# Soft-capped attention with a soft mixture of experts: queries and keys cast by transfers, more exponential tiles on VectorE, side jobs moved

## The chip, the core and the metric

The kernel runs on one NeuronCore of a Trainium2 chip. The core has TensorE (matmuls into PSUM), ScalarE (activation functions), VectorE and GpSimd (elementwise work) and SyncE, which here only issues transfers. The engines run their own instruction streams in order and wait for each other by semaphores. [...] The metric is the device time of one execution in microseconds (us). The traces name the engines PE (PEld for its weight loads), ACT, DVE, POOL and SP.

## The reference

For each of 8 batches and 12 heads, attention over 448 tokens of width 64, with scores capped by a tanh; then a soft mixture of 8 experts with 4 slots each over all 3584 tokens.

```
scores = cap * tanh((q @ k.T / 8) / cap)            # cap = 30
attn = exp(scores - max); attn /= sum + 1e-9
x = (attn @ v), heads side by side                   # 3584 x 768
logits = x @ phi                                     # 3584 x 32 slots
d = softmax of logits over tokens;  slot_input = d.T @ x
slot_out[e] = relu(slot_input[e] @ w1[e]) @ w2[e]
out = softmax of logits over slots @ slot_out        # 3584 x 768 f32
```

## The kernel before

**Attention.** Two heads that lie 64 rows apart on TensorE make a pair, two pairs a "quad" (four heads), three quads a batch: NQ = 24 quads, 48 pairs. A pair's scores are cut into 7 tiles of 128 x 448, 336 in all, worked off in 56 chunks of CH = 6 tiles. A batch is 7 chunks; "step n" of batch b is chunk 7b+n, n from 0 to 6.

For each chunk j the main loop (L523) emits: two tanh over three tiles each, from PSUM (`tanh_chunk`, L278); the exponential of an earlier chunk in place (`exp_chunk`, L282); the value pass of a pair, in two halves (`pv_pass`: 14 matmuls of L318, then on VectorE a reciprocal L328 and a product L329); and the scores of the next chunk, two groups of six matmuls (`qk_chunk`, L269). Since 48 pairs fall on 56 chunks, one step in seven (step 2) has no value pass. Exponential tiles have four buffers, so the tanh of chunk j+1 overwrites the buffer of chunk j-3. Scores have two buffers of three banks, the value pass one bank (psV), everything else one bank (psT, tag T).

**Preparation of a quad.** q and k come in as f32 by transfers from SyncE (`load`), VectorE casts them to bf16 (`cast`, L226), TensorE turns them by 7 transposes of 128 x 128 (`transp`, L237) and VectorE copies the result from PSUM (L239). v is cast on GpSimd in two halves (`vcast`, L247 and L248), as soon as the value passes of the quad two before are done.

**Side jobs.** For each batch: transposes of the attention output x (`x_transp`, L344 and L346), logits (L355, L360), the exponential of the logits (`e_exp`, L366), a copy of it on GpSimd (`e_rep`, L372), its transposes (`e_transp`, L391 and L392), the sum over tokens (`e_norm`, L379 and L383), slot sums (L407) and, every second batch, the reciprocal of sums over slots (`e_sums`, L401 and L402). `spare(n)` issues n filler matmuls (L506). All these have a place by hand: `at(j, slot, job)` puts a job in chunk j at slot 0 (ahead of the tanh), a (after the first half of the value pass), b (after the first scores), c (after the second half of the value pass) or d (after the second scores).

**Shared exponentials.** In the chunks listed in `shared` (L289) VectorE computes the exponential of tile 0 by a polynomial (`poly_exp`, L294 to L304) in three parts at slots a, c and d of the same chunk; ScalarE then does only five tiles.

**Weights.** w1 and w2 (f32) are loaded and cast by transfers from GpSimd, spread over slot b of the chunks (`wjobs`); the part of w2 that doesn't fit goes to DRAM as bf16 and is loaded back (`w2t`, L631) into memory that the attention frees.

**The end.** After the attention come the two expert layers (L649, L676) and the output: the first 10 token tiles are stored in two halves of 384 columns each (`half_tile`, L702 to L707), the first halves while the second layer still runs; the others as whole rows, ScalarE and VectorE taking turns.

Of the kernel before, what the change touches and what calls it, by code (L numbers as in the profile page):

```python
# [9 lines left out]
F32 = mybir.dt.float32  # L10
BF16 = mybir.dt.bfloat16
# [5 lines left out]
P = 128  # L17
HP = 64
NT = 7
DH = 64  # L20
S = 448
# [11 lines left out]
def kernel(  # L33
# [54 lines left out]
    slacc = consts.tile([P, NJ, NS], F32, name="slacc")  # L88

    w1b = [wts.tile([P, NJ, F], BF16, name=f"w1b{e}", tag="w1", bufs=E)  # L90
           for e in range(E - 1)]
    w2b = wts.tile([P, R2, D], BF16, name="w2b")


# [32 lines left out]

    att = ExitStack()
    ld = att.enter_context(tc.tile_pool(name="ld", bufs=1))
    cst = att.enter_context(tc.tile_pool(name="cst", bufs=1))  # L130
    ldv = att.enter_context(tc.tile_pool(name="ldv", bufs=1))
    qk = att.enter_context(tc.tile_pool(name="qk", bufs=2))
    vb = [att.enter_context(tc.tile_pool(name="vb0", bufs=1))]
# [22 lines left out]
                       ap=[[NT * DH, P], [2 * S * DH, 2], [1, NT * DH]])  # L156

    def raw_tile(nm):
        return (ldv if nm == "v" else ld).tile([P, 2, S], F32, name=nm + "raw",
                                               tag=nm + "raw")  # L160

    def load(nm, Q):
        if Q < NQ:
            t = raw_tile(nm)
            sp.dma_start(out=t, in_=quad_ap(nm, Q))
            raws[nm, Q] = t

    def load_first():

        for nm in "qkv":  # L170
            raws[nm, 0] = raw_tile(nm)
        kc = raws["k", 0].rearrange("p h (c d) -> p h c d", d=DH)
        kin = quad_ap("k", 0, 0).rearrange("p (c d) -> p c d", d=DH)
        sp.dma_start(out=raws["q", 0][:, 0, :], in_=quad_ap("q", 0, 0))
        for c0, c1 in ((0, CS), (CS, NT)):
            act.dma_start(out=kc[:, 0, c0:c1, :], in_=kin[:, c0:c1, :])
        for nm in "kq":
            sp.dma_start(out=raws[nm, 0][:, 1, :], in_=quad_ap(nm, 0, 1))
        t = wts.tile([P, 3, 2, S], F32, name="raw1", tag="w1", bufs=E)
        for n, nm in enumerate("kqv"):  # L180
            raws[nm, 1] = t[:, n, :, :]
            if nm == "v":
                sp.dma_start(out=raws["v", 0], in_=quad_ap("v", 0))
            sp.dma_start(out=raws[nm, 1], in_=quad_ap(nm, 1))

    def first_pieces(h, jobs):

        for stage, nm, c0, c1, eng, bank, at0 in jobs:
            copy = act.copy if eng is act else dve.tensor_copy
            cols = slice(h * HP, h * HP + HP)  # L190
            if stage == "cast":
                copy(casts[nm, 0][:, c0:c1, cols],
                     raws[nm, 0][:, h, c0 * DH:c1 * DH].rearrange("p (c d) -> p c d", d=DH))
            elif stage == "turn":
                for c in range(c0, c1):
                    pe.transpose(bank[cols, at0 + c - c0, :], casts[nm, 0][:, c, cols], ident)
            else:
                copy(qkT[nm, 0][cols, c0:c1, :], bank[cols, at0:at0 + c1 - c0, :])

    def first_half(h):  # L200
        for nm in ("k", "q"):
            if h == 0:
                casts[nm, 0] = cst.tile([P, NT, P], BF16, name=nm + "bf", tag=nm + "bf")
                qkT[nm, 0] = qk.tile([P, NT, P], BF16, name=nm + "T", tag=nm + "T")
        one = psT.tile([P, 8, P], BF16, name="ps1", tag="T")
        two = psV.tile([P, NT, P], BF16, name="ps2", tag="pv")
        if h == 0:

            first_pieces(h, (("cast", "k", 0, CS, dve, None, 0), ("cast", "q", 0, 4, dve, None, 0),
                             ("cast", "q", 4, NT, act, None, 0), ("turn", "k", 0, CS, pe, two, 0),  # L210
                             ("copy", "k", 0, CS, dve, two, 0), ("turn", "q", 0, 4, pe, one, 0),
                             ("cast", "k", CS, NT, act, None, 0),
                             ("copy", "q", 0, 4, dve, one, 0), ("turn", "q", 4, NT, pe, two, CS),
                             ("copy", "q", 4, NT, act, two, CS), ("turn", "k", CS, NT, pe, one, 4),
                             ("copy", "k", CS, NT, dve, one, 4)))
        else:
            first_pieces(h, (("cast", "k", 0, NT, dve, None, 0), ("cast", "q", 0, NT, dve, None, 0),
                             ("turn", "k", 0, NT, pe, two, 0), ("turn", "q", 0, NT, pe, one, 0),
                             ("copy", "k", 0, NT, dve, two, 0), ("copy", "q", 0, NT, dve, one, 0)))
            for nm in ("q", "k"):  # L220
                raws.pop((nm, 0)), casts.pop((nm, 0))
                load(nm, 2)

    def cast(nm, Q):
        t = cst.tile([P, NT, P], BF16, name=nm + "bf", tag=nm + "bf")
        dve.tensor_copy(t.rearrange("p c (h d) -> p h c d", h=2),  # L226
                        raws.pop((nm, Q)).rearrange("p h (c d) -> p h c d", d=DH))
        casts[nm, Q] = t
        if Q > 1:
            load(nm, Q + 1)  # L230

    def transp(nm, Q):
        src = casts.pop((nm, Q))
        home = (psV, "pv") if (nm, Q) == ("k", 1) else (psT, "T")
        ps = home[0].tile([P, NT, P], BF16, name=nm + "ps", tag=home[1])
        for c in range(NT):
            pe.transpose(ps[:, c, :], src[:, c, :], ident)  # L237
        t = qk.tile([P, NT, P], BF16, name=nm + "T", tag=nm + "T")
        dve.tensor_copy(t, ps)  # L239
        qkT[nm, Q] = t  # L240
# [45 lines left out]

    shared = [j for j in range(NCH - 2) if j % 7 == 3 and j > 7] if cap < 80 else []  # L289

    def poly_exp(j, part):
        t, bits = exs[j][:, 0, :], 2.0 ** 23
# [146 lines left out]

    def quad_in(Q, cast_k, cast_q, k_in, q_in, v_in):  # L440
        if 0 < Q < NQ:
            at(*cast_k, cast, "k", Q)
            at(*cast_q, cast, "q", Q)
            at(*k_in, transp, "k", Q)
            at(*q_in, transp, "q", Q)
            at(*v_in, vcast, Q)

    for b in range(B):
        j = b * PER
        if b == 0:  # L450
            quad_in(1, (0, "a"), (0, "b"), (0, "d"), (1, "a"), (2, "d"))
        else:
            quad_in(3 * b + 1, (j - 1, "b"), (j, "a"), (j - 1, "d"), (j, "c"), (j + 1, "d"))
        quad_in(3 * b + 2, (j + 1, "c"), (j + 2, "c"), (j + 2, "b"), (j + 2, "d"),
                (j + 4, "d"))
        quad_in(3 * b + 3, (j + 4, "a"), (j + 5, "a"), (j + 4, "d"), (j + 5, "c"),
                (j + 6, "d"))
        p = 6 * b
        at(j + 1, "d", spare, 34 if b == 0 else 10)
        at(j + 2, "d" if b == 0 else "a", spare, 4 if b == 0 else 14)  # L460
        if b:
            at(j + 2, "c", spare, 8)
        at(j + 3, "d", spare, 10)
        at(j + 4, "a", x_transp, p)
        at(j + 5, "a", x_transp, p + 1)
        at(j + 6, "a", x_transp, p + 2)
        at(j + 5, "d", logits, 3 * b)
        if b < B - 1:
            at(j + 7, "a", x_transp, p + 3)
            at(j + 8, "a", x_transp, p + 4)  # L470
            at(j + 7, "d", logits, 3 * b + 1)
            at(j + 9, "a", x_transp, p + 5)
            at(j + 9, "d", logits, 3 * b + 2)
            at(j + 11, "0", e_exp, b)
            at(j + 11, "d", slot_sums, b)
            if b < B - 2:
                at(j + 12, "d", e_transp, b)
            if b < B - 2:
                at(j + 13, "d", e_norm, b)
            if b % 2:  # L480
                at(j + 14, "d", e_sums, b // 2)
    for j in shared:
        for dj, slot, part in ((0, "a", 0), (0, "c", 1), (0, "d", 2)):
            at(j + dj, slot, poly_exp, j, part)
    for n, job in enumerate(wjobs):
        at(1 + n * (NCH - 5) // len(wjobs), "b", *job)
    for j, slot, n in ((0, "a", 10), (0, "c", 10), (1, "b", 10), (1, "c", 8)):
# [208 lines left out]
    def half_tile(n, half, home, eng):  # L696

        if n % 8 == 0:
            obs[n, half] = wts.tile([P, 8, HD], F32, name="obh", tag="w1", bufs=E)
        ob = obs[n - n % 8, half][:, n % 8, :]  # L700
        bb, c = divmod(n, NT)
        pe.matmul(home, et_tile(bb, c), so[half], start=True, stop=True)  # L702
        if eng == "dve":
            dve.tensor_scalar_mul(ob, home, winv[:, bb, c:c + 1])
        else:
            act.mul(ob, home, winv[:, bb, c:c + 1])
        store(n, half, half + 1, ob)  # L707
# [10 lines left out]
    for n0 in range(0, n2, 4):  # L718
        layer2(n0, 1)
        if n0 >= 4 and n0 % 8 == 4 and done < NH - 2:  # L720
            for eng in ("act", "dve"):
                half_tile(done, 0, bank([P, HD], name="op0"), eng)
                done += 1
    dve.tensor_copy(so[1], so_ps[1])
    for n in range(done, NH):
# [68 lines left out]
```

The softmax here doesn't subtract the row's maximum and nothing guards it: scores larger than these inputs give would overflow.

## Time and profile before

| | |
|---|---|
| time, three runs | 317.34 to 318.18 us, median 318.17 |
| span of the profiled run | 314.8 us |
| attention | up to some 269 us |
| tanh, L278 | 113 instructions, 162.3 us busy |
| exponentials, L282 | 58 instructions, 159.2 us busy |
| casts of q and k on VectorE, L226 | 46 instructions, two of 128x896 per quad |
| casts of v on GpSimd, L247 and L248 | 24 each, some 0.93 and 0.96 us |
| VectorE's polynomial, L294 to L304 | 7 chunks, seven instructions each |
| filler matmuls, L506 | 470 |

A row of the groups reads: line, engine, operation, output and input with their shapes, count, busy time and mean duration, idle time before it and what ended it. Busy times on ScalarE overlap, so two of its rows can add up to more than the time that they took. In the listing in order of time a row has its start, its length, the engine, the line and, in brackets, the idle time before it and what ended that. In the chain of work that ended last a piece has start, length and what it was.

### The profile page before, as it was taken

What the parts mean: (1) busy time and instruction counts of PE and PEld (TensorE: products, weight loads), DVE (VectorE), ACT (ScalarE), POOL (GpSimd) and SP (SyncE); (2) the same over time, 40 slices, a digit from 0 to 9 for tenths busy, and PEclk for the clock granted to TensorE, in tenths of its full rate; (3) what the DMA queues carried; (4) which work ended last, traced back from release to release, by engine and by line L of the source; (5) the groups of instructions that cost most, each with busy time, mean ns of one, the idle gap of its engine ahead of it and who ended that gap; (6) DMA issues with size and microseconds to landing.
All of it is one profiled execution on the core that took longest, in us unless ns stands there. A gap on an engine that the chain in (4) does not pass through costs nothing.

```text
span 314.8 us, 8844 instructions
## 1 busy us (share of the span) xinstructions
PE 269.4 (86%) x3804; PEld 191.0 (61%) x3804; DVE 193.7 (62%) x473; ACT 281.3 (89%) x208; POOL 106.5 (34%) x134
## 2 busy tenths in 40 slices
PE   7899898899889998898889989898889998998720
PEld 6667665667666665666666666666666677743400
DVE  3636565766586659575867587657766574327840
ACT  4999999999999999999999999999999999326730
POOL 2464342523543452354245416441732130200000
PEclk9999999999999999999999999999999999999985
DMA  8899999799999999999999999999999807898997
GB/s 223 267 234 238 291 244 269 159 231 256 235 210 231 266 237 207 254 220 266 194 225 269 221 264 190 242 235 266 209 232 254 214 14 207 290 393 301 389 411 314
DMA packets 57479, 77.68 MB, mean 247 GB/s; under 512 B 3809, under 2 KB 53601, under 8 KB 57441
## 3 DMA queue, kind: packets, MB, share of 16 engines
q0 software_dynamic: 30480, 25.22, 52.1%
q1 hardware_dynamic: 26672, 51.68, 48.1%
q8 instruction: 29, 0.48, 0.6%
q10 hardware_dynamic: 288, 0.23, 0.2%
q14 instruction: 10, 0.07, 0.1%
HBM read 91.32 MB, written 18.87 MB: 350 GB/s over the span
## 4 chain that ended last, share of the span: by engine, by line
ACT 67%; PE 20%; DVE 5%; issue 3%; DMA 2%; DVEq 0%; ACTq 0%
ACT ex L278 33%; ACT ex L282 32%; PE pv L318 5%; PE sc L269 3%; PE so_ps L676 2%; PE junk L506 2%; PE hp L649 2%; ACT ob L754 1%; PE op L702 1%; DMA kraw<-in_k_dram 1%; DVE xq L329 1%; PE op L745 1%; PE xps L344 1%; DMA out_dram<-obh 1%; DVE ob L752 1%
## 5 line engine op out<-in xcount | busy, mean ns | idle before, releaser
L278 ACT ACTIVATE ex<-sc 128x1344 bf16<-128x1344 f32 (+1 forms) x113 | 162.3, 1693 | 0.9 <-PE sc L269 0.8
L282 ACT ACTIVATE ex<-ex 128x2688 bf16<-128x2688 bf16 (+4 forms) x58 | 159.2, 2779 | 0.1
L318 PEld LDWEIGHTS <-ex 128*128 128x128 bf16 x1344 | 78.7, 97 | 21.5 <-DVE xq L329 17.8
L318 PE MATMUL pv<-vbd,ex 128*128 128x130 bf16 x1274 | 88.6, 220 | 2.6 <-ACT ex L282 0.7
L269 PE MATMUL sc<-qT,kT 64*64 64x448 bf16 x672 | 78.6, 358 | 8.2 <-ACT ex L278 7.9
L247 POOL CAST vbd<-vraw 64x896 bf16<-64x896 f32 x23 | 21.5, 936 | 103.6 <-PE pv L318 65.3
L269 PEld LDWEIGHTS <-kT 64*64 64x64 bf16 x672 | 27.3, 105 | 25.3 <-issue 7.5
L329 DVE TENSOR_TENSOR xq<-pv,rec 128x256 bf16<-128x256 f32 x91 | 38.6, 424 | 3.1
L328 DVE RECIPROCAL rec<-pv 128x4 f32<-128x4 f32 x91 | 16.5, 181 | 32.1 <-PE pv L318 31.2
L506 PEld LDWEIGHTS <-ones 128*128 128x128 bf16 x470 | 28.6, 100 | 11.6 <-DVE xq L329 8.0
L372 POOL COPY e<-E 128x512 bf16<-128x512 bf16 x9 | 7.2, 795 | 81.5 <-ACT E L366 49.6
L506 PE MATMUL junk<-ones 128*128 128x128 bf16 x433 | 31.4, 219 | 2.5 <-DVE xq L329 1.6
L239 DVE COPY kT<-kps 128x896 bf16<-128x896 bf16 x23 | 14.4, 625 | 24.6 <-PE kps L237 24.4
L109 POOL DMA_DIRECT2D w1b<-in_moe_w_dram x32 | 25.2, 791 | 0.0
L248 POOL CAST vbd<-vraw 64x896 bf16<-64x896 f32 x23 | 23.7, 1029 | 1.3
L346 DVE COPY xT<-xps 128x512 bf16<-128x512 bf16 x47 | 19.5, 415 | 3.2 <-PE xps L344 3.0
L344 PE MATMUL xps<-ident,xq 128*128 128x128 bf16 x188 | 18.1, 218 | 0.2 <-DVE zacc L383 0.2
L239 DVE COPY qT<-qps 128x896 bf16<-128x896 bf16 x23 | 14.2, 616 | 5.2 <-PE qps L237 5.2
L226 DVE CAST kbf<-kraw 128x896 bf16<-128x896 f32 x22 | 16.0, 728 | 1.3 <-DMA kraw<-in_k_dram 1.3
L237 PE MATMUL kps<-ident,kbf 128*128 128x128 bf16 x161 | 12.8, 219 | 4.2 <-DVE slacc L418 2.2
L237 PE MATMUL qps<-ident,qbf 128*128 128x128 bf16 x161 | 12.8, 219 | 3.2 <-DVE lg L360 2.7
L237 PEld LDWEIGHTS <-kbf 128*128 128x128 bf16 x161 | 10.0, 97 | 9.0 <-issue 8.3
(113 smaller groups left out, 255.5 us busy)
## 6 DMA issues: line engine op xcount, KB each, us to landing
w1b<-in_moe_w_dram POOLq DMA_DIRECT2D x32, 384.0 KB, 10.2
vraw<-in_v_dram SPq DMA_DIRECT2D x23, 448.0 KB, 6.6
qraw<-in_q_dram SPq DMA_DIRECT2D x22, 448.0 KB, 7.8
kraw<-in_k_dram SPq DMA_DIRECT2D x22, 448.0 KB, 6.0
w2d<-in_moe_w_dram POOLq DMA_DIRECT2D x20, 384.0 KB, 9.2
w2t<-w2d SPq DMA_DIRECT2D x20, 384.0 KB, 5.9
out_dram<-ob SPq DMA_DIRECT2D x8, 768.0 KB, 7.3
w2b<-in_moe_w_dram POOLq DMA_DIRECT2D x12, 384.0 KB, 9.9
```

The costliest lines, as they stand in the source:

```text
L109: pool.dma_start(out=w1b[e][:, js, fs], in_=w1r[:, e, js, fs])
L237: pe.transpose(ps[:, c, :], src[:, c, :], ident)
L239: dve.tensor_copy(t, ps)
L247: pool.tensor_copy(t[0:HP, :, :, 0:DH], raw[0:HP])
L248: pool.tensor_copy(t[HP:P, :, :, DH + 1:VW - 1], raw[HP:P])
L269: pe.matmul(sc[cs, u, 0:S], qkT["k", Q][r, c, cs], qkT["q", Q][r, :, cs], start=True, stop=True)
L278: act.activation(exs[j][:, half * CS + u0:half * CS + u1, :], sc[:, u0:u1, 0:S], ACT.Tanh, scale=qk_scale / cap)
L282: act.activation(exs[j][:, u0:u1, :], exs[j][:, u0:u1, :], ACT.Exp, scale=cap)
L318: pe.matmul(pvs[pr, half][:, n, 0:VW], exs[j][:, u, GOFF[g]:GOFF[g] + P], vbds[Q % 2][:, h, c, :], start=(c == 0 and n == 0), stop=(c == N ...
L329: dve.tensor_tensor(xq[Q][:, 2 * half:2 * half + 2, h * P:(h + 1) * P] .rearrange("p g (i d) -> p g i d", i=2), pv[:, :, :, 0:DH], rec.to_ ...
L344: pe.transpose(ps[:, g, :], xq[Q][:, g, h * P:(h + 1) * P], ident)
L506: pe.matmul(junk if home is None else home, ones, ones, start=True, stop=True)
```

## The change

Four things. (1) From the third quad on, q and k are cast to bf16 by the transfers themselves, issued from GpSimd into two buffers each; VectorE's casts remain for the first two quads, whose bf16 tiles lie in a weight buffer. The transposes read the loaded layout directly: 14 of 128 x 64 per tensor in place of 7 of 128 x 128. (2) The polynomial takes a tile in 16 chunks (steps 1 and 3 of each batch from chunk 8 on, and chunks 3 and 54) in place of 7; its third part moves to the next chunk. (3) Side jobs move: k of the third quad is turned one chunk earlier, e transposes, token sums and sums over slots three, three and two chunks later, and the fillers at steps 1, 2 and 3 shrink from 10, 14 and 10 to 6, 12 and 4. (4) The first half output tile is computed into two PSUM banks of 192 columns, scaled by ScalarE and VectorE side by side. It is meant to take exponential work from ScalarE, make room for it on VectorE, keep TensorE's side work spread out, and let the first store go earlier.

```diff
@@ loads and casts
-    cst = att.enter_context(tc.tile_pool(name="cst", bufs=1))
...
     def raw_tile(nm):
-        return (ldv if nm == "v" else ld).tile([P, 2, S], F32, name=nm + "raw",
-                                               tag=nm + "raw")
+        if nm == "v":
+            return ldv.tile([P, 2, S], F32, name="vraw", tag="vraw")
+        return ld.tile([P, 2, S], BF16, name=nm + "b", tag=nm + "raw", bufs=2)
 
     def load(nm, Q):
         if Q < NQ:
             t = raw_tile(nm)
-            sp.dma_start(out=t, in_=quad_ap(nm, Q))
+            (sp if nm == "v" else pool).dma_start(out=t, in_=quad_ap(nm, Q))
             raws[nm, Q] = t
...
-    def cast(nm, Q):
-        t = cst.tile([P, NT, P], BF16, name=nm + "bf", tag=nm + "bf")
-        dve.tensor_copy(t.rearrange("p c (h d) -> p h c d", h=2),
-                        raws.pop((nm, Q)).rearrange("p h (c d) -> p h c d", d=DH))
-        casts[nm, Q] = t
-        if Q > 1:
-            load(nm, Q + 1)
+    def cast(nm):
+
+        dve.tensor_copy(casts[nm, 1].rearrange("p c (h d) -> p h c d", h=2),
+                        raws.pop((nm, 1)).rearrange("p h (c d) -> p h c d", d=DH))
 
     def transp(nm, Q):
-        src = casts.pop((nm, Q))
+        src = casts.pop((nm, Q)) if Q == 1 else raws.pop((nm, Q))
...
         for c in range(NT):
-            pe.transpose(ps[:, c, :], src[:, c, :], ident)
+            if Q == 1:
+                pe.transpose(ps[:, c, :], src[:, c, :], ident)
+                continue
+            for h in range(2):
+                pe.transpose(ps[h * HP:h * HP + HP, c, :], src[:, h, c * DH:(c + 1) * DH], ident)
@@ shared exponentials
-    shared = [j for j in range(NCH - 2) if j % 7 == 3 and j > 7] if cap < 80 else []
+    shared = [j for j in range(NCH) if j % 7 in (1, 3) and j > 7 or j in (3, NCH - 2)] if cap < 80 else []
@@ places of the jobs
         if 0 < Q < NQ:
-            at(*cast_k, cast, "k", Q)
-            at(*cast_q, cast, "q", Q)
+            for nm, when in (("k", cast_k), ("q", cast_q)):
+                at(*when, *((cast, nm) if Q == 1 else (load, nm, Q + 1)))
...
-        quad_in(3 * b + 2, (j + 1, "c"), (j + 2, "c"), (j + 2, "b"), (j + 2, "d"),
+        quad_in(3 * b + 2, (j, "d"), (j + 1, "c"), (j + 2, "b"), (j + 2, "d"),
                 (j + 4, "d"))
-        quad_in(3 * b + 3, (j + 4, "a"), (j + 5, "a"), (j + 4, "d"), (j + 5, "c"),
+        quad_in(3 * b + 3, (j + 4, "a"), (j + 5, "a"), (j + 3, "d"), (j + 5, "c"),
                 (j + 6, "d"))
-        at(j + 1, "d", spare, 34 if b == 0 else 10)
-        at(j + 2, "d" if b == 0 else "a", spare, 4 if b == 0 else 14)
+        at(j + 1, "d", spare, 34 if b == 0 else 6)
+        at(j + 2, "d" if b == 0 else "a", spare, 4 if b == 0 else 12)
...
-        at(j + 3, "d", spare, 10)
+        at(j + 3, "d", spare, 10 if b == 0 else 4)
...
             if b < B - 2:
-                at(j + 12, "d", e_transp, b)
-            if b < B - 2:
-                at(j + 13, "d", e_norm, b)
+                at(j + 15, "d", e_transp, b)
+                at(j + 16, "d", e_norm, b)
             if b % 2:
-                at(j + 14, "d", e_sums, b // 2)
+                at(j + 16, "d", e_sums, b // 2)
     for j in shared:
-        for dj, slot, part in ((0, "a", 0), (0, "c", 1), (0, "d", 2)):
-            at(j + dj, slot, poly_exp, j, part)
+        for slot, part in (("a", 0), ("c", 1)):
+            at(j, slot, poly_exp, j, part)
+        at(j + 1, "b" if j % 7 == 1 else "a", poly_exp, j, 2)
@@ half_tile
+        if n == half == 0:
+
+            for p, (bank_p, mul) in enumerate(zip(home, (act.mul, dve.tensor_scalar_mul))):
+                cs = slice(p * HD // 2, (p + 1) * HD // 2)
+                pe.matmul(bank_p, et_tile(bb, c), so[half][:, cs], start=True, stop=True)
+                mul(ob[:, cs], bank_p, winv[:, bb, c:c + 1])
+            store(n, half, half + 1, ob)
+            return
```

## The prediction

> **What bounds the kernel now.** I read the busy shares first, then the chain of work that ended last, then the waits, and then one batch in order of time.
>
> ```profile
> PE 269.4 (86%) x3804; PEld 191.0 (61%) x3804; DVE 193.7 (62%) x473; ACT 281.3 (89%) x208; POOL 106.5 (34%) x134
> ```
>
> ScalarE is busiest, and in each 32.6 us stretch of the attention it is busy for all 32.6. The chain shows what one chunk costs it (start, us, what):
>
> ```profile
> 185.09 2.33 ACT ex L282
> 187.62 2.36 ACT ex L278 x2
> 189.99 1.96 ACT ex L282
> ```
>
> Two tanh (2.36 us) and one exponential: 2.33 us for six tiles, 1.96 where VectorE takes one of the six. That is 0.37 us per tile handed over. The waits say who leans on whom (total us, times, longest):
>
> ```profile
> ACT ex L278 <- PE sc L269: 0.8, 1, 0.8
> ```
> ```profile
> PE sc L269 <- ACT ex L278: 7.9, 19, 0.7
> ```
>
> ScalarE waits for TensorE once, at the start; TensorE waits for ScalarE 19 times. So ScalarE sets the end of the attention, and 0.37 us per tile is won as long as TensorE stays ahead. How far ahead is the question. I call chunk 7b+n "step n" of batch b. TensorE in steps 1 to 3 of batch 5:
>
> ```profile
> 175.95 0.98 PE L318 MATMUL pv<-vbd,ex 128*128 128x130 bf16 x14
> ...
> 178.24 0.39 PE L344 MATMUL xps<-ident,xq 128*128 128x128 bf16 x4
> ...
> 179.33 0.75 PE L269 MATMUL sc<-qT,kT 64*64 64x448 bf16 x6
> ...
> 182.78 0.96 PE L318 MATMUL pv<-vbd,ex 128*128 128x130 bf16 x14
> 183.96 0.75 PE L269 MATMUL sc<-qT,kT 64*64 64x448 bf16 x6 [0.22 <-ACT ex L278]
> ```
> ```profile
> 186.90 3.09 ACT L278 ACTIVATE ex<-sc 128x1344 bf16<-128x1344 f32 x2
> ```
>
> Step 2 has no value pass (L318), so side jobs sit there. The last line is step 4's two tanh. Recorded starts on ScalarE run early late in the span, but ends agree with TensorE (it takes a score bank 0.04 us after a tanh ends), so I count from ends: the pair ends at 189.99, its first member at 188.81, and needs 1.2 us, so must begin at 187.61. It writes an exponential buffer last read by step 3's second value pass (four buffers). That pass could start at 184.48, when the first pass's norm is done, and end at 185.45: **2.16 us of slack**.
>
> [...] here the 128*32 matmuls of L649 take 1.41 us for 24 of 512 columns, a quarter of serial. [...]
>
> ```profile
> 187.53 0.62 DVE L303 SCALAR_TENSOR_TENSOR xp<-xp,xm 128x448 f32<-128x448 f32 x1
> 187.75 0.87 POOL L372 COPY e<-E 128x512 bf16<-128x512 bf16 x1 [7.07 <-ACT E L366]
> ...
> 188.19 0.91 DVE L304 SCALAR_TENSOR_TENSOR ex<-xp,xe 128x448 bf16<-128x448 f32 x1
> ```
>
> The copy takes 0.87 us, not 0.61 as when alone; L304 takes 0.91, not the 0.63 of its shortest run. Each starts in effect 0.14 us before the other ends[...]. Casts of v do the same:
>
> ```profile
> 177.06 0.93 POOL L247 CAST vbd<-vraw 64x896 bf16<-64x896 f32 x1 [4.74 <-PE pv L318]
> ...
> 177.53 0.94 DVE L226 CAST kbf<-kraw 128x896 bf16<-128x896 f32 x1
> ...
> 178.04 1.24 POOL L248 CAST vbd<-vraw 64x896 bf16<-64x896 f32 x1
> ```
>
> **The change part by part.**
>
> *Sixteen shared chunks instead of seven.* ScalarE saves 9 x 0.37 = 3.35 us. VectorE pays 9 x 3.66 us (shortest runs of L294 to L304), 33 us.
>
> *Casts in transfers.* 44 VectorE casts go (L226, 16.0 + 14.5 = 30.5 us), so its total is nearly unchanged; 67% of a batch is no bound. GpSimd issues 44 more transfers at about 0.77 us (L109), 34 us beside 106 of busy time: hidden. The engines of the transfers carry the same reads. A transfer from GpSimd lands 10.2 us after issue (median; longest 16.0, third in a burst). I put the tightest, the k load of step 4, some 12 us ahead of its transposes and leading its burst: no cost.
>
> *Twice as many transposes, of half the columns.* [...] If they pair as L649's do, 14 take some 0.03 us more than 7 (0.55); if serial, 0.39 more. I take 0.03. Twelve fillers fewer per batch return 12 x 0.057 = 0.7 us (ten take from 177.67 to 178.24).
>
> *Side jobs moved.* Steps 5 and 6 lose the e transposes and the normaliser sum, so TensorE enters step 1 at its limit, the free score bank (scores at 174.58, when a tanh had ended, instead of 175.37): its second value pass starts 0.8 us earlier against ScalarE than in batch 5 above. But step 1 is now crowded on VectorE. Count from the end of that pass (176.93 above). Norm to 0.66. The v cast waits for the same pass and starts at 0.13, ending at 1.06; the first two-input polynomial step (L300) gets in at 0.92 and ends at 1.53; [...] the next step (L301) ends at 2.84, and only then comes the copy of the e transposes, to 3.22. There is one side-job bank in PSUM (tag T), so step 2's x transposes wait until 3.28; behind them in TensorE's queue stand 12 fillers and the scores, at 4.27. Before, the scores came at 179.33 - 176.93 = 2.40. Later by 1.87, less 0.8: **1.1 us**.
>
> In step 2, from scores to the next value pass took 182.78 - 179.33 = 3.45. Now: k transposes 0.69 to 1.27, VectorE's copy to 1.92, the third polynomial part (0.66 + 0.63) to 3.13, and behind it the sum's addition (3.22), logits (0.35) and addition (0.3) to 3.94, q transposes, value pass at 4.4: **1.0 us** more. After odd batches the reciprocal of e sums adds another 0.62 (in the trace, 173.44 to 174.06). Against a start that ScalarE's own saving in step 2 makes 0.37 us earlier, lateness is 1.1 + 1.0 + 0.37 = 2.5 us, odd 3.1, against 2.16: ScalarE stalls **0.35** or **0.95**.
>
> In step 3 the k transposes, moved there, have their copy behind the second polynomial part; step 4's x transposes wait for that copy. By the same counting, step 4's second value pass is another 0.3 us late. This holds for batches 2 to 7 (0 and 1 have no e transposes to place): 3 x 0.65 + 3 x 1.25 = **5.7 us**.
>
> *First output tile in two halves.* The first store leaves after half an L706 (0.58): some 0.25 us earlier, and transfers are full from then on. The smaller cast pool lets one less weight reload start early (about 1 us of transfer), which fits into the 1.7 us hole before the first store.
>
> Sum: 318.17 - 3.35 - 0.25 + 5.7 = **320.3 us**.
>
> **The rivals.**
>
> *The saving lands.* VectorE's slack takes it all: 318.17 - 3.6 + 0 to 0.6, about **314.9**. For it: VectorE has 10 us idle per batch (busy 22.14 of 32.70), steps 5 and 6, tightest before, are relieved, and without the collision of L300 and L301 with the v cast (0.95 us) the 2.16 us nearly suffice. Against: the collision follows from one and the same value pass.
>
> *Half of it.* Only the odd batches and step 4 stall, 3 to 4 us: **318.0**.
>
> *TensorE becomes the bound.* Serial transposes put 3 x 0.39 us more into steps 2 and 3: some 7 us over six batches, **327**. Against: L649, and the scores (L269), which overlap by pairs.
>
> *Keys come late*, behind bursts of weights in one queue: a few us, **323**. Against: the lead of 12 us.
>
> **How the numbers follow.** Forecast 0.40; saving lands 0.36; half 0.16; TensorE 0.05; late keys 0.03. Faster is the second, same the third, slower the rest, 0.48. The lateness of one batch is known to some 0.4 us, so six batches to 2.4: up to 322.8; down, the full saving, 314.4.
>
> **What the profile would show.** Right: ScalarE's L278 waiting for pv (L318) in steps 4 and 5 of batches 2 to 7, 0.3 to 1 us each; TensorE's L344 waiting for the ET copy (L392), about 2 us in step 2; L301 near 1.2 us and not 0.63 in step 1; exponentials of 1.96 us 16 times. Wrong: if ScalarE waits for nothing, the saving lands; if kps and qps groups of 14 take 0.95 us, transposes are serial; if transposes wait for transfers, the queue is the cause. I would be wrong above all if VectorE reached L300 before the v cast starts, or if the buffer were free before the pass ends.

## The result and the profile after

The changed kernel takes **338.19 us** (median of four executions, 334.0 to 342.59) against 318.18 (317.34 to 319.43): a ratio of 1.053, 95% interval 1.044 to 1.062. The forecast was 320.3 and its range ended at 322.8. Executions more than 1.5% over the fastest of their kernel are left out of the ratios, and since these are mostly the ones in which TensorE's clock fell furthest, the median of such a kernel says more than its ratio. Lines of the changed kernel are those of the kernel before plus 8 (tanh L286, exponential L290, value pass L326, x transposes L352, L400 the "ET copy", which takes the e transposes out of PSUM).

Busy time first, then two rows of slices from the same page, for the changed kernel:

```profile
PE 295.2 (87%) x4029; PEld 203.6 (60%) x4029; DVE 199.2 (58%) x493; ACT 279.5 (82%) x208; POOL 137.4 (40%) x178
```
```profile
ACT  4999999999499989998699858999999759514730
PEclk9999999997599979995799757999999559999995
```

The clock row of the kernel before:

```profile
PEclk9999999999999999999999999999999999999985
```

ScalarE's total fell by 1.8 us, but it now has holes, and they lie where the clock row shows something new: digits of 5 and 7, where before it was 9 throughout the attention. The clock that TensorE is granted falls to half again and again. The clock record of this execution (start and length in us) says how long:

```
81.6 13.7   122.6 3.4   153.3 13.7   190.9 17.1   262.5 17.1     (all at 0.5 of full)
```

That is 64.9 us of the attention at half clock, in pieces of 1, 4 or 5 times 3.41 us. The kernel before had none, up to 304 us. The chain of work that ended last, by engine, before and after:

```profile
ACT 67%; PE 20%; DVE 5%; issue 3%; DMA 2%; DVEq 0%; ACTq 0%
```
```profile
ACT 39%; PE 38%; DVE 15%; issue 2%; DMA 2%; DVEq 0%; SPq 0%; ACTq 0%
```

The waits of the changed kernel (total us, times, longest):

```profile
ACT ex L286 <- PE pv L326: 17.7, 12, 3.3
...
PE xps L352 <- DVE ET L400: 10.2, 6, 2.3
...
ACT ex L286 <- PE sc L277: 8.6, 7, 1.8
```

The forecast's two signs are there: ScalarE waits for a value pass twelve times, eleven of them in steps 4 and 5 of batches 2 to 7 (one, of 0.2 us, is in batch 0), and the x transposes wait for the ET copy six times. But the twelve come to 17.7 us where it had 5.7, and seven waits for scores stand beside them, where there was one. Batch 2 in order of time (start, length, then engine and line) shows the start of it on VectorE and GpSimd:

```profile
77.93 1.03 POOL L255 CAST vbd<-vraw 64x896 bf16<-64x896 f32 x1 [3.26 <-PE pv L326]
...
78.64 0.80 DVE L308 SCALAR_TENSOR_TENSOR xp<-xm 128x448 f32<-128x448 f32 x1
...
79.02 1.24 POOL L256 CAST vbd<-vraw 64x896 bf16<-64x896 f32 x1
...
79.47 1.26 DVE L309 SCALAR_TENSOR_TENSOR xp<-xp,xm 128x448 f32<-128x448 f32 x1
...
80.66 0.38 DVE L400 COPY ET<-eps 128x448 bf16<-128x448 bf16 x1
```

and what TensorE does meanwhile and after it:

```profile
78.42 0.40 PE L399 MATMUL eps<-ident,e 128*128 128x128 bf16 x4
78.78 0.51 PE L514 MATMUL junk<-ones 128*128 128x128 bf16 x6
81.08 0.38 PE L352 MATMUL xps<-ident,xq 128*128 128x128 bf16 x4 [1.79 <-DVE ET L400]
81.31 1.18 PE L514 MATMUL junk<-ones 128*128 128x128 bf16 x12
82.42 1.33 PE L277 MATMUL sc<-qT,kT 64*64 64x448 bf16 x6
83.67 0.96 PE L245 MATMUL kps<-ident,kb 128*64 128x128 bf16 x14
```

The second value pass of step 1 ended at 77.79. Counted from there the ET copy ends at 3.25 (forecast 3.22) and the x transposes begin at 3.29 (forecast 3.28); L309 takes 1.26 us, 0.63 at its shortest, and the half of the v cast beside it (L256) 1.24 where the median is 0.96. The forecast's count had the two lengthen each other, an estimate from such pairs in the trace before; why they do isn't shown. Up to here the forecast is right to 0.03 us. Then TensorE, idle for 1.79 us, comes back to a granted clock of 0.50: six score matmuls take 1.33 us and not 0.76, 14 half transposes 0.96 and not 0.58. The table by stretches of 3.4 us has PE busy second and the granted clock in the third column from the right:

```profile
74.80:78.20 3.40, 3.01 (x43) 2.20 (x42) 2.31 (x8) 3.40 (x4) 0.27 (x1) 1.00 1.21 235
78.20:81.60 3.40, 1.60 (x24) 1.13 (x21) 2.86 (x6) 3.40 (x3) 3.34 (x4) 1.00 1.25 205
81.60:85.00 3.40, 3.40 (x35) 2.13 (x33) 0.66 (x2) 3.40 (x3) 0.90 (x2) 0.50 1.17 256
85.00:88.40 3.40, 2.77 (x32) 1.62 (x32) 1.90 (x5) 1.78 (x3) 0.00 (x0) 0.50 1.23 207
```

A stretch with TensorE busy 1.60 of 3.40 us, and the next one is at 0.50. Coming back takes longer: TensorE is busy for 3.40, 2.77, 3.40 and 3.40 us of the four stretches from 81.6, and yet the clock stays at half until 95.3. One comparison lies in the execution itself: batch 6 has the same jobs as batches 2 and 4 but no stretch at half clock, and ScalarE loses 0.3 us there (counted as in the table below), where it loses 5.1 and 5.2 us in those two. So the theory to test: **a stretch of some 3.4 us with little work on TensorE halves its clock; ScalarE then waits for passes that take 1.70 us in place of 0.97** (the 14 matmuls from 88.95 against those from 76.82). The rivals: it is the thinner fillers; it is the casting transfers; or the waits that the forecast counted are simply longer, and the clock is an effect.

### The profile page after: what moved, and what is told of

It is laid out like the page before. It is cut to its first block, busy times and chain, and to the rows that moved or that the text cites. A ratio compares the mean times of both kernels' runs of the same rounds, so it can differ in the third digit from the quotient of the medians.

```text
span 340.8 us, 9280 instructions
## 1 busy us (share of the span) xinstructions
PE 295.2 (87%) x4029; PEld 203.6 (60%) x4029; DVE 199.2 (58%) x493; ACT 279.5 (82%) x208; POOL 137.4 (40%) x178
## 4 chain that ended last, share of the span: by engine, by line
ACT 39%; PE 38%; DVE 15%; issue 2%; DMA 2%; DVEq 0%; SPq 0%; ACTq 0%
ACT ex L286 19%; ACT ex L290 19%; PE pv L326 11%; PE sc L277 8%; PE junk L514 4%; PE kps L245 2%; DVE xq L337 2%; DVE xp L309 2%; PE qps L245 2%; PE so_ps L684 2%; DVE xp L308 2%; PE hp L657 2%; DMA out_dram<-ob 2%; PE xps L352 1%; DVE xm L304 1%
## 5 line engine op out<-in xcount | busy, mean ns | idle before, releaser
L286 ACT ACTIVATE ex<-sc 128x1344 bf16<-128x1344 f32 (+1 forms) x113 | 140.9, 1316 | 26.3 <-PE pv L326 17.7
L290 ACT ACTIVATE ex<-ex 128x2688 bf16<-128x2688 bf16 (+4 forms) x58 | 133.5, 2305 | 0.1
L326 PE MATMUL pv<-vbd,ex 128*128 128x130 bf16 x1274 | 97.5, 231 | 4.2 <-ACT ex L290 2.4
L326 PEld LDWEIGHTS <-ex 128*128 128x128 bf16 x1344 | 84.8, 103 | 26.9 <-DVE xq L337 13.5
L277 PE MATMUL sc<-qT,kT 64*64 64x448 bf16 x672 | 87.2, 390 | 3.6 <-ACT ex L286 2.1
L514 PEld LDWEIGHTS <-ones 128*128 128x128 bf16 x386 | 27.1, 110 | 7.8 <-issue 3.3
L352 PE MATMUL xps<-ident,xq 128*128 128x128 bf16 x188 | 18.4, 221 | 11.1 <-DVE ET L400 10.2
L256 POOL CAST vbd<-vraw 64x896 bf16<-64x896 f32 x23 | 23.6, 1028 | 1.3
L352 PEld LDWEIGHTS <-xq 128*128 128x128 bf16 x188 | 13.1, 98 | 12.3 <-issue 12.3
L245 PEld LDWEIGHTS <-kb 128*64 128x64 bf16 x308 | 11.4, 128 | 10.8 <-issue 10.8
L167 POOL DMA_DIRECT2D qb<-in_q_dram x22 | 16.2, 737 | 3.6 <-DMA kraw<-in_k_dram 3.2
L245 PE MATMUL qps<-ident,qb 128*64 128x128 bf16 x308 | 14.7, 242 | 2.9 <-DVE lg L368 2.9
```

The source lines that it names most:

```text
L245: pe.transpose(ps[h * HP:h * HP + HP, c, :], src[:, h, c * DH:(c + 1) * DH], ident)
L256: pool.tensor_copy(t[HP:P, :, :, DH + 1:VW - 1], raw[HP:P])
L277: pe.matmul(sc[cs, u, 0:S], qkT["k", Q][r, c, cs], qkT["q", Q][r, :, cs], start=True, stop=True)
L286: act.activation(exs[j][:, half * CS + u0:half * CS + u1, :], sc[:, u0:u1, 0:S], ACT.Tanh, scale=qk_scale / cap)
L290: act.activation(exs[j][:, u0:u1, :], exs[j][:, u0:u1, :], ACT.Exp, scale=cap)
L326: pe.matmul(pvs[pr, half][:, n, 0:VW], exs[j][:, u, GOFF[g]:GOFF[g] + P], vbds[Q % 2][:, h, c, :], start=(c == 0 and n == 0), stop=(c == N ...
```

## The experiments

From the profiled execution of seven of the kernels, in us: the attention from the first tanh to the end of the last exponential, ScalarE's lost time in it, the time of it at half clock, and the span after it. Lost time is counted from ends, as in the prediction: by how much each instruction of ScalarE ends later than the one before it plus the usual time (the median) of its shape. The changed kernel's is its longest execution, 342.59 us.

| | attention | ScalarE lost in it | at half clock | after it |
|---|---|---|---|---|
| before | 262.4 | 0.5 | 0 | 45.6 |
| changed | 286.1 | 27.7 | 64.9 | 47.5 |
| 1: e jobs back | 259.1 | 0.7 | 0 | 46.6 |
| 3: gap filled | 274.3 | 15.9 | 27.3 | 48.5 |
| 5: gap and chain filled | 265.5 | 7.0 | 0 | 48.1 |
| 10: transfers alone | 262.2 | 0.3 | 0 | 46.0 |
| 11: tiles alone | 269.8 | 11.3 | 0 | 47.8 |

The attention less the lost time is 261.9 us in the two rows with 7 tiles on VectorE and 258.4 or 258.5 in the five with 16. So the saving of 3.4 us was there in every one of these, the changed kernel too; the rest of the differences in the attention is waiting.

**1. The e jobs (e transposes, token sums, sums over slots) back at their old places**, all else as changed.

```diff
-                at(j + 15, "d", e_transp, b)
-                at(j + 16, "d", e_norm, b)
+                at(j + 12, "d", e_transp, b)
+                at(j + 13, "d", e_norm, b)
             if b % 2:
-                at(j + 16, "d", e_sums, b // 2)
+                at(j + 14, "d", e_sums, b // 2)
```

> The changed kernel with the e transposes, token sums and sums over slots at their old places (steps 5, 6 and 0); all else as changed. Gap theory: in step 2 the x transposes wait 1.8 us for the copy of the e transposes, and this idle TensorE both delays the value passes and lets the clock fall to half; without it there is no such wait, the clock stays at 1.0 up to the last 15 us, and the time is 315 to 317. Filler theory (the clock falls because 12 fillers per batch are gone): clock still falls, 330 or more. Transfer theory (late keys, a fuller GpSimd): 330 or more.

Measured: **314.55 us** (314.03 to 315.79) against 317.41, ratio 0.991 (0.988 to 0.994); clock 0.981 to 0.987 in all eight executions; a little under the range expected. Its waits of ScalarE inside the attention are down to the one at the start:

```profile
ACT ex L286 <- PE sc L277: 0.8, 1, 0.8
```

So the move of three small jobs is worth 23.6 us, and without it the change does what it was made for: it beats both kernels. It doesn't yet say by what mechanism.

**2. The fillers back at 10, 14 and 10**, all else as changed.

```diff
-        at(j + 1, "d", spare, 34 if b == 0 else 6)
-        at(j + 2, "d" if b == 0 else "a", spare, 4 if b == 0 else 12)
+        at(j + 1, "d", spare, 34 if b == 0 else 10)
+        at(j + 2, "d" if b == 0 else "a", spare, 4 if b == 0 else 14)
...
-        at(j + 3, "d", spare, 10 if b == 0 else 4)
+        at(j + 3, "d", spare, 10)
```

> The changed kernel with the fillers of steps 1, 2 and 3 at 10, 14 and 10 again. Gap theory: the wait in step 2 shrinks by only 0.23 us (four fillers ahead of it), so it stays at 1.6 us and the clock still falls in some batches: 325 to 342. Filler theory: clock at 1.0, 318 or less.

Measured: 335.31 us (332.1 to 335.98), ratio 1.053 (1.046 to 1.060), clock 0.927 in the profiled execution. Six waits for the ET copy remain, 9.4 us in all. The thinner fillers aren't the cause; experiment 9 asks the same from the other side.

**3. The gap filled**: 30 spare matmuls in place of 6 where TensorE waits for the ET copy.

```diff
-        at(j + 1, "d", spare, 34 if b == 0 else 6)
+        at(j + 1, "d", spare, 34 if b == 0 else 6 if b == 1 else 30)
```

> The changed kernel with 30 fillers instead of 6 at the end of step 1 in batches 2 to 7: 24 x 0.057 = 1.4 us of matmuls inside the wait, which they don't lengthen. This parts the two costs. Gap theory: the clock stays at 1.0, the waits of ScalarE for the value passes in steps 4 and 5 remain at 0.3 to 1 us each, and the time is what was forecast without a clock: 318 to 321. If the waits alone made the loss, 330 or more at a full clock. Filler theory: also a full clock, so told apart by the run with 10, 14 and 10.

Measured: 328.94 us (323.33 to 331.56), clock 0.942 in the profiled execution; a miss. Waits for the ET copy fell to 2.9 us, and the clock still fell, in five batches. Where it fell first, TensorE in order of time:

```profile
117.14 0.25 PE L387 MATMUL zps<-ones,e 128*128 128x1 bf16 x4
117.95 0.31 PE L409 MATMUL wps<-ones,ET 128*128 128x1 bf16 x7 [0.56 <-DVE zacc L391]
118.56 0.35 PE L363 MATMUL lps<-phib,xT 128*128 128x32 bf16 x8 [0.30 <-DVE winv L410]
119.30 0.58 PE L245 MATMUL qps<-ident,qb 128*64 128x128 bf16 x14 [0.38 <-DVE lg L368]
```

and the stretches by 3.4 us:

```profile
117.20:120.60 3.40, 2.16 (x49) 1.94 (x47) 1.82 (x5) 3.40 (x3) 0.00 (x0) 1.00 1.23 213
120.60:124.00 3.40, 3.40 (x30) 1.98 (x27) 2.42 (x7) 1.25 (x3) 2.21 (x3) 0.51 0.88 132
```

Filling one hole had left another: in step 2 the sums, the logits and the q transposes use the one side-job bank in turn, so each waits for a VectorE copy of the one before. No gap there is over 0.6 us, but the stretch is busy for 2.16 of 3.40 us only, and again the next one is at half clock. The gap need not be one piece.

**4. The second polynomial part of step 1 behind the e transposes**, so that the ET copy doesn't queue behind L308 and L309.

```diff
-        for slot, part in (("a", 0), ("c", 1)):
+        for slot, part in (("a", 0), ("d" if j % 7 == 1 else "c", 1)):
```

> The changed kernel with the second polynomial part of step 1 behind the e transposes in VectorE's queue (slot d instead of c); nothing else moves. Gap theory: the copy of the e transposes comes at once, the part no longer meets the v cast, L309 near 0.63 us: wait in step 2 under 0.3 us, clock at 1.0, 315 to 318. Filler and transfer theories: 330 or more.

Measured: 322.02 us, with twelve executions in two groups: five from 316.65 to 318.17 (clock 0.973 to 0.979), as expected or nearly so, and seven from 320.5 to 325.3 (0.941 to 0.962), which were not. In the profiled one, of the faster group, the wait for the ET copy is gone; the chain of experiment 3 is not, and the clock falls once after it, for 3.4 us. That it falls more often in the slower group is likely from their clocks, but none of them has a trace. Within this one kernel the time follows the clock: from 0.979 and 316.8 us to 0.941 and 325.3, 8.5 us for 0.038.

**5. Gap and chain filled**: experiment 3, and six spare matmuls behind each of the sums and the logits of step 2.

```diff
             at(j + 9, "d", logits, 3 * b + 2)
+            if b:
+                at(j + 9, "d", spare, 6)
...
                 at(j + 16, "d", e_norm, b)
+                at(j + 16, "d", spare, 6)
             if b % 2:
                 at(j + 16, "d", e_sums, b // 2)
+                at(j + 16, "d", spare, 6)
```

> The changed kernel with the wait for the ET copy filled (30 spare matmuls, as in the third experiment) and six more spare matmuls each behind the Z sums, the e sums and the logits of step 2 in batches 2 to 7, where TensorE otherwise goes through four short operations that each wait for a VectorE copy. If what brings the clock down is a stretch of 3.4 us with little work on TensorE, whatever makes the gap, and the third experiment had left one such stretch (117.2 to 120.6 us, busy 0.64): no half clock in the attention (mean 0.975 or more), and the time is what the waits alone cost, 318 to 321 us, the forecast. If the clock falls for another reason than a thin stretch: mean at most 0.95 and 326 us or more.

Measured: **321.41 us** (320.93 to 322.5) against 317.51, ratio 1.013 (1.011 to 1.015), clock 0.982 to 0.985: the clock as expected, the time 0.4 us over the range. Busy time, clock row, waits and one stretch of this version:

```profile
PE 283.5 (88%) x4263; PEld 200.0 (62%) x4263; DVE 199.7 (62%) x493; ACT 278.9 (87%) x208; POOL 136.8 (43%) x178
```
```profile
PEclk9999999999999999999999999999999999999985
```
```profile
ACT ex L286 <- PE pv L326: 5.4, 11, 1.1
```
```profile
78.20:81.60 3.40, 2.95 (x49) 2.56 (x46) 2.87 (x5) 3.40 (x3) 3.34 (x4) 1.00 1.25 204
```

This is the run that decides. *More* matmuls that compute nothing make the kernel 16.8 us faster, with every job of the change in its order. No dependency was taken away; the last line is the stretch of batch 2 that was busy 1.60 us, now 2.95, and the clock stays. The clock is therefore a cause and not an effect, and what is left are the waits of the forecast, in steps 4 and 5 of batches 2 to 7: ten of these eleven, 5.2 of the 5.4 us.

**6. The kernel before with the e jobs moved**, nothing else.

```diff
-                at(j + 12, "d", e_transp, b)
+                at(j + 15, "d", e_transp, b)
...
-                at(j + 13, "d", e_norm, b)
+                at(j + 16, "d", e_norm, b)
...
-                at(j + 14, "d", e_sums, b // 2)
+                at(j + 16, "d", e_sums, b // 2)
```

> The kernel before with only the e transposes, the Z sums and the e sums moved to where the change has them (steps 1 and 2 of the batch after next); tiles handed over, casts, spare matmuls as before. If the late place of these jobs alone makes the thin stretch: clock under 0.96 and 322 us or more. If it takes both, the late place and a tile on VectorE in step 1 whose second part holds up the ET copy: the copy follows its transposes at once, no stretch of 3.4 us under 0.7 busy, clock 0.98 and 317 to 319.5 us.

Measured: 320.79 us (318.73 to 322.95), ratio 1.009 (1.005 to 1.013), clock 0.972 to 0.982. Between the two expectations: the late place alone costs 1 to 5 us. The profiled execution (318.77) never falls to half clock in the attention, waits for the ET copy 1.3 us in all, and its attention is as long as before, 262.6 us; what it loses comes after it. Where the slower executions lose is not recorded. To lose 20 it takes the tiles on VectorE as well.

**7. Only the e transposes back**, sums late as in the change.

```diff
-                at(j + 15, "d", e_transp, b)
+                at(j + 12, "d", e_transp, b)
```

> The changed kernel with only the e transposes put back five steps earlier; Z sums and e sums stay late, in step 2. Tells the two halves of the pile apart. If the gap behind the ET copy is what counts: 315 to 317.5 us, clock 0.98, ScalarE waits for the pass of the chunk under 2 us in all. If the chain of short jobs in step 2 is enough: clock under 0.96, and 320 us or more.

Measured: 320.73 us, but from 316.02 (clock 0.978) to 326.25 (0.938) over eight executions. Neither expectation as written: the gap behind the ET copy is the larger half (17.5 us of the medians come back with it), and the chain alone leaves a time that varies with the clock, as in experiment 4.

**8. Six more tiles on VectorE**, in step 5, on top of experiment 1.

```diff
-    shared = [j for j in range(NCH) if j % 7 in (1, 3) and j > 7 or j in (3, NCH - 2)] if cap < 80 else []
+    shared = [j for j in range(NCH) if j % 7 in (1, 3, 5) and j > 7 or j in (3, NCH - 2)] if cap < 80 else []
```

(third parts of step 5 at slot b of step 6)

> The first experiment's version (e jobs back at their old places) with six more tiles on VectorE, those of step 5 from batch 1 on, 22 in all. With 0.37 us saved by each, as in the forecast, and no new wait: 312.3 us. If step 5 has no room (two x transposes, q transposes and a value cast have copies on VectorE there): ScalarE waits for passes by 0.3 us or more in most of the six batches, 314 to 317 us; with the clock falling as well, 320 or more.

Measured: 329.67 us (328.31 to 330.02), ratio 1.037 (1.034 to 1.040), clock 0.945 to 0.960. The third of the expectations. Its step 5 is the same picture in another place; TensorE, in order of time:

```profile
165.75 0.76 PE L277 MATMUL sc<-qT,kT 64*64 64x448 bf16 x6
167.71 0.38 PE L399 MATMUL eps<-ident,e 128*128 128x128 bf16 x4 [1.20 <-DVE qT L247]
169.20 0.38 PE L363 MATMUL lps<-phib,xT 128*128 128x32 bf16 x8 [1.11 <-DVE ET L400]
```

The first wait is for the copy of the q transposes, which stood behind the norm; the second for the ET copy, which stood behind L308 and L309. From 165.8 to 169.2 TensorE is busy a third of the time, and the clock is halved from 169.2.

**9. The kernel before with the thinner fillers** (6, 12, 4), nothing else.

> The kernel before with the spare matmuls thinned exactly as the change thins them (6, 12 and 4 in place of 10, 14 and 10 in batches 1 to 7) and nothing else. The forecast counted these 12 per batch only as 0.7 us of TensorE time given back, off the path: no change, 317 to 318.2 us. If the spare matmuls as such hold the clock, so that thinning them is what brought it down in the changed kernel: stretches of 3.4 us under 0.7 busy, clock under 0.97, 321 us or more.

Measured: 317.53 us against 317.42, ratio 0.999 (0.997 to 1.001), clock 0.977 to 0.986. The fillers were costed rightly, and the rival that they hold the clock in this kernel falls.

**10. The changed kernel with tiles and e jobs as before**: left are the casting transfers (with one early weight tile fewer), the half transposes, the earlier k transposes, the thinner fillers and the first output tile over two banks.

```diff
-    shared = [j for j in range(NCH) if j % 7 in (1, 3) and j > 7 or j in (3, NCH - 2)] if cap < 80 else []
+    shared = [j for j in range(NCH - 2) if j % 7 == 3 and j > 7] if cap < 80 else []
```

(and the diff of experiment 1)

> The changed kernel with the e jobs and the tiles of VectorE as before (7 tiles of step 3): left of the change are the casting transfers with their 14 half transposes, the thinner spare matmuls and the first output tile over two banks. By the forecast's terms (transfers at no cost, two banks 0.25 us): 317.2 us, at a clock of 0.98. If the casting transfers cost something of their own (late keys, half transposes one after the other): 319 us or more, with TensorE waiting for transfers or groups of 14 at 1.1 us.

Measured: 317.37 us against 317.42, ratio 1.000 (0.998 to 1.003), clock 0.978 to 0.986. What is left costs nothing in sum, and by itself brings nothing. Its transposes, groups by line (count, busy us, mean ns):

```profile
L245 PE MATMUL qps<-ident,qb 128*64 128x128 bf16 x308 | 12.8, 222 | 2.7 <-DVE lg L368 2.7
```

These 308 half transposes, 22 groups of 14, take 12.8 us; the 161 full ones of the kernel before, 23 groups of 7, took 12.8 as well. So the halves run in pairs: in the trace of the changed kernel, at full clock, they start two at a time (18.947 and 18.950, then 19.027 and 19.030 us).

**11. The kernel before with the 16 tiles**, casts on VectorE.

```diff
-    shared = [j for j in range(NCH - 2) if j % 7 == 3 and j > 7] if cap < 80 else []
+    shared = [j for j in range(NCH) if j % 7 in (1, 3) and j > 7 or j in (3, NCH - 2)] if cap < 80 else []
```

(third parts in the next chunk, as in the change)

> The kernel before with only the 16 tiles on VectorE and their third parts in the next step; casts on VectorE, e jobs and spare matmuls as before. By the forecast's term of 0.37 us for each of 9 tiles: 314.2 us against 317.5. If VectorE needs the relief of the casting transfers to carry them (casts of 1.2 us ahead of copies that TensorE waits for): waits of TensorE for copies, the clock under 0.97 and 319 us or more.

Measured: 327.05 us (326.26 to 330.38), ratio 1.032 (1.027 to 1.038), clock 0.978 to 0.987. VectorE needs the relief, and the waits for copies came as expected, but not the fall of the clock. Its waits:

```profile
PE qps L237 <- DVE lg L360: 8.5, 7, 1.2
ACT ex L278 <- PE pv L318: 6.7, 12, 0.7
```

In step 2 the third polynomial part and then the cast of q (0.62 us) stand ahead of the addition of the logits, and the q transposes wait for their bank up to 1.2 us. Tiles alone +9.6 us, transfers alone 0, both together (experiment 1) -2.9: these two parts of the change pay only together. A total of VectorE's work wouldn't show that; even with the tiles alone it is busy for 70% of the span.

**12. The 22 tiles with the e transposes a step later**, in step 6, and the Z sums (over tokens) in step 0.

```diff
-                at(j + 12, "d", e_transp, b)
-                at(j + 13, "d", e_norm, b)
+                at(j + 13, "d", e_transp, b)
+                at(j + 14, "d", e_norm, b)
```

> The 22 tiles again, with the e transposes a step later (step 6) and the Z sums in step 0, where no tile's second part stands on VectorE ahead of the ET copy. If the ET copy behind the second part in step 5 is what made the thin stretch of the 22-tile version: the clock back at 0.98, 312 to 314 us. If step 5 has no room for a tile whatever is moved: clock under 0.96, 319 us or more.

Measured: 322.79 us (320.17 to 325.53), ratio 1.014 (1.008 to 1.020), clock 0.952 to 0.975. 6.9 us come back and the clock falls once (6.8 us) where it fell five times, but the hoped-for 312 isn't there: ScalarE still waits 5.7 us for scores and passes. Which job of steps 5 and 6 is in the way stays open.

**All traces together.** For each of the 14 profiled kernels I cut 40 to 288 us into stretches of 3.413 us on the raster of its own clock record (from first change to last, all lie multiples of 3.413 us apart; the pieces of 13.653, 3.413 and 17.067 us in the changed kernel's are 4, 1 and 5 of them), and took the share of each in which TensorE had a matmul running; then I counted after which the clock fell from full to half:

```
busy share of the stretch   stretches at full clock   followed by half clock
under 0.6                        14                        11
0.6 to 0.8                      105                        11
over 0.8                        844                         0
```

All 22 falls follow a stretch at 0.32 to 0.76; the five of the changed kernel stand behind 0.47, 0.75, 0.43, 0.32 and 0.59. The share doesn't decide alone: one at 0.49 passed, and experiment 11 goes through stretches of 0.64 or 0.65 thirteen times without a fall, where experiment 3 fell after 0.64. What else decides stays open.

## Why the prediction was wrong

**The sign was right, the size was not**: 20.0 us slower where 2.1 were forecast.

*What held.* The saving on ScalarE: exponentials of 2.33 and 1.96 us in the chain of the changed kernel too, and 3.4 us less ScalarE time in every row of the table with 16 tiles (forecast 3.35). VectorE as no bound by its total: 199 of 341 us. GpSimd's issues hidden, keys in time, half transposes in pairs: experiment 10, 317.37 us against 317.42, 12.8 us for the half transposes as for the full ones, and no wait of transposes for a transfer. The fillers off the path: experiment 9. The count through step 1: 3.25 and 3.29 for 3.22 and 3.28. Where the clock holds (experiment 5) it goes on being right: scores at 81.98, so 4.26 after the pass (forecast 4.27), next value pass at 86.48, 4.50 later (forecast 4.4). From ends, ScalarE loses 6.3 us there in batches 2 to 7 for the forecast's 5.7; batch by batch the agreement is looser, 1.5 to 1.7 in the odd ones (forecast 1.25) and 0.3, 0.3 and 1.1 in the even ones (forecast 0.65), so some of it is luck. Experiment 5 as a whole, 321.4, is inside the prediction's range.

*The step that failed* is the one on lateness: "Later by 1.87, less 0.8: 1.1 us", then "from scores to the next value pass", and from them the term of 5.7 us. All its durations came from a trace at full clock, and what the waits themselves do to the clock was put at nothing, without a reason. It even named TensorE's wait ("about 2 us in step 2") and priced it as lateness alone. In the changed kernel the next value pass came at 88.95, 6.5 us after the scores and not 4.4, with six scores at 1.33 us and 14 transposes at 0.96. The term measured 17.7 us in waits for passes, with 8.6 for scores beside it. Of the median's 20.0 us, 16.8 go with the clock (experiment 5 against the changed kernel). The rest is near the forecast in size but not in place: in the profiled execution of experiment 5 the attention is 3.1 us longer than before (forecast 5.7 - 3.35 = 2.35) and the span after it 2.5 us longer (forecast -0.25).

An estimate from the slope of experiment 4 comes out alike: 8.5 us for 0.038 of mean clock, so some 15 us for the fall from 0.983 to the changed kernel's median of 0.914.

*Smaller misses.* The first output tile over two banks: the first store is issued 14.55 us after the last exponential in place of 14.66, the last one 35.36 in place of 35.44 (experiment 10 against before); 0.1 us and not 0.25. The tile of chunk 54 was not costed at the end: after the last exponential the first copy of x waits 3.1 us in the changed kernel and in experiment 11, where the kernel before and experiment 10, without that tile, wait 1.6. Experiment 1 has the tile and waits 2.1, so the tile isn't all of it; the rest stays open.

*The rivals.* "TensorE becomes the bound" came nearest, but for a reason that experiment 10 rules out, serial transposes. "The saving lands", 314.9, is what experiment 1 gives, 314.55: it would have been true with the e jobs left where they were.

## What to carry to other kernels

When a change makes TensorE wait, price the wait twice: as lateness, and as a stretch in which TensorE is little busy. Divide the time around it into stretches of 3.4 us, the step of the clock records here; in these kernels 11 of 105 stretches from 0.6 to 0.8 and 11 of 14 under 0.6 were followed by a fall, and what followed ran at half clock for 3.4 to 17.1 us in the changed kernel, longer than the wait itself (2.3 us at most). Where a job can't move, try spare matmuls *in* the waits: with the wait for the ET copy and the chain of step 2 filled the mean clock was 0.982 to 0.985 (experiment 5), with the first alone 0.942 to 0.973 (experiment 3), with the fillers back at their old numbers 0.923 to 0.942 (experiment 2). And a short PSUM copy that TensorE waits for is better ahead of the long polynomial parts in VectorE's queue, whatever VectorE's total says: placed so, the median fell from 338.19 to 322.02 us (experiment 4).

## What was not expected of the hardware

The share of half clock differs between executions of the same kernel: 316.02 to 326.25 us at a mean clock of 0.978 to 0.938 for experiment 7, 316.65 to 325.33 at 0.979 to 0.941 for experiment 4, while experiments 1, 5 and 9 keep within 0.6%. In these kernels a spread of 3% with a clock that varies with it came in versions with thin stretches left; two versions of the same speed in their best executions are not equally good. Not every spread is the clock: four of 28 executions of the kernel before, measured beside experiments 9 to 12, took 319.6 to 320.2 us at 0.983, and what lengthens those is not known.
